# A new opening for an FFT-filter and feed-forward kernel: input by two queues, weight conversion in three steps, filter rows as 16 KB runs

One core of a Trainium2 chip. The metric is the device time of one execution in microseconds (us); lower is better. All runs quoted here are of the fast state (none had the lower clock or the longer time of the slow one), and every kernel's output was correct. Times of stages and of single waits come from one profiled execution of each kernel.

## The reference

```python
def _attn_ref(x, filt_r, filt_i):            # x (8, 3008, 256) f32; filters (1505, 256) f32
    X = np.fft.rfft(x, axis=1)
    Y = X * (filt_r + 1j * filt_i)[None, :, :]
    return np.fft.irfft(Y, n=x.shape[1], axis=1).astype(np.float32)

def _moe_ref(x, w_in, w_out):                # x (24064, 256); w_in (256, 2048), w_out (2048, 256): float64
    h = x @ w_in
    g = np.where(h > 0.0, h, np.exp(np.minimum(h, 0.0)) - 1.0)
    return (g @ w_out).astype(np.float32)

def reference(x, filt_r, filt_i, moe_w_in, moe_w_out):
    return _moe_ref(_attn_ref(x, filt_r, filt_i).reshape(8 * 3008, 256), moe_w_in, moe_w_out)
```

The weights arrive as float64. No engine multiplies them as such: the kernel takes the two 32-bit words of each number apart and builds a float32 ("conversion", sixteen pieces of 128x512 numbers).

## The kernel before

The length 3008 is 47 x 64, and the transform goes in two stages by matrix products. For each batch:

- x is read with its mirrored rows; VectorE makes sums and differences (`x_unit`), TensorE the first stage (`a_unit`), ScalarE evicts (copies the product from PSUM, where TensorE writes it, to SBUF), SyncE writes the result z to DRAM (`z_write`).
- z is read back, transposed on the way (`z_read`). In eight groups TensorE makes the second stage, VectorE multiplies by the filter (four products of 128x512), GpSimd adds the products in two sums, and TensorE goes back (`b_unit`, `bi_unit`).
- y goes through DRAM too, and after the "n-stage" (`n_unit`) the feed-forward loop runs over 192 "quads" of work, in which TensorE is full.

Batch 0 has nothing to hide behind: the *opening*. The same opening loads the whole filter into one tile `ff` and converts the weights. Its parts, with the lines "..." for what is cut:

```python
def x_load(b, c, queue=nc.sync, place=None):       # all on SyncE but the table
    ...
    queue.dma_start(w, ta_d[:, 2 * c:2 * c + 2, :])
    for h in range(2):
        ...
        nc.sync.dma_start(t[r]..., raw(x, b * N + i, [[N1 * D, 32], [32 * N1 * D, 2], [1, 2 * D]]))   # 2 KB runs
        for u in range(2):
            ...
            nc.sync.dma_start(t[r, :, u, :], raw(x, b * N + N1 - i - u, ...))                       # 1 KB runs, mirrored

def z_write(b, c):
    ...
    for r in range(2):
        nc.sync.dma_start(z[r], t[HALVES[r]])                                                       # 1 KB runs

def f_read_first(t, a):                            # the filter, by GpSimd's queue
    r = a * 64
    for c, src in enumerate((filt_r, filt_i)):
        nc.gpsimd.dma_start(t[r:r + 24, :, c, :, :]..., raw(src, 2 * a, [[64 * D, 24], [4 * D, NG], [1, 2 * D]]))  # 2 KB runs
        ...                                        # mirrored rows, 1 KB runs

def b_unit(b, g, f=None):
    ...
    nc.vector.tensor_tensor(out=sr, in0=re, in1=f[:, 0], op=ALU.mult)      # and si, p, q
    nc.gpsimd.tensor_tensor(out=sr, in0=sr, in1=p, op=ALU.subtract)
    nc.gpsimd.tensor_tensor(out=si, in0=si, in1=q, op=ALU.add)

def w_convert(k):                                  # one block
    nc.vector.tensor_scalar(out=m, in0=hi, scalar1=0x000FFFFF, ...)        # mantissa
    nc.scalar.activation(out=l, in_=lo, func=AXT.Identity, scale=2.0 ** -52)
    nc.scalar.activation(out=f, in_=m, func=AXT.Identity, scale=2.0 ** -20, bias=1.0)
    nc.vector.tensor_scalar(out=e, ...)            # three tensor_scalars: exponent
    ...
    nc.vector.scalar_tensor_tensor(out=e, ...)     # sign
    nc.vector.tensor_tensor(out=f, in0=f, in1=l, op=ALU.add)
    ...                                            # product, and four sums after every second piece

# the opening
for k in range(2):
    w_fetch(k)
for c in range(NXC):
    x_load(0, c, nc.scalar, ...)
nc.gpsimd.memset(ff, 0.0)
...
wait_x(3); w_fetch(2); w_fetch(3); wait_x(5)       # GpSimd held back until x is there
for a in range(2):
    f_read_first(ff, a)
for c in range(NXC):
    x_unit(0, c); a_unit(0, c); z_write(0, c)
    if c in (0, 2):
        w_convert(c // 2)
...                                                # z_read, then eight groups with w_convert(6..11) between
```

Of the kernel before, what the change touches and what calls it, by code (L numbers as in the profile page):

```python
# [22 lines left out]
N1 = 47  # L23
# [12 lines left out]
FBUFS = 3  # L36
LO, HI = slice(0, 48), slice(64, 112)
# [3 lines left out]
def _make_tables():  # L41










    n2, k2 = np.arange(N2), np.arange(K2)
    ta, tn = np.zeros((P, H, P)), np.zeros((P, H, P))
    for i in range(H):
        for h in range(2):
            if h and i == 0:
                continue
            n1 = N1 - i if h else i
            th = 2 * np.pi * (((N1 * n2[:, None] + n1) * k2[None]) % N) / N
            c, s = np.cos(th), -np.sin(th)  # L60
            c[:, 0], s[:, 0] = 1.0, 1.0 - 2.0 * (n2 % 2)
            sign = -1.0 if h else 1.0
            r = slice(h * 64, h * 64 + 64)
            for p, v in enumerate((c, sign * s, s, sign * c)):
                ta[r, i, p * 32:p * 32 + 32] = v
                tn[p * 32:p * 32 + 32, i, r] = v.T
    tb = ta.reshape(2, 2, 32, NXC, 2, 2, 4, 16, 2)[:, 0].transpose(3, 0, 1, 2, 4, 7, 5, 6)
    ta = np.ascontiguousarray(tb).reshape(P, H // 2, P)
    i = np.arange(H)[:, None]
    gb, gr, gi = (np.zeros((P, 2, 64)) for _ in range(3))  # L70
    q = np.arange(N1)[None]
    th = 2 * np.pi * ((i * np.where(q < 24, q, 70 - q)) % N1) / N1
    c, s = np.cos(th), np.sin(th)
    sign = np.where(q < 24, 1.0, -1.0)
    gb[0:24, 0, :N1], gb[24:48, 0, :N1] = c, s
    gb[64:88, 0, :N1], gb[88:112, 0, :N1] = c * sign, -s * sign
    for o in (0, 64):
        gr[o:o + N1, 0, 0:24], gr[o:o + N1, 0, 24:48] = 2 / N * c.T, 2 / N * s.T
        gi[o:o + N1, 0, 0:24], gi[o:o + N1, 0, 24:48] = 2 / N * (c * sign).T, -2 / N * (s * sign).T
    k1 = np.arange(24)[None]  # L80
    t0 = 2 * np.pi * ((i * k1) % N1) / N1
    t3 = 2 * np.pi * ((i * (32 + 64 * k1)) % N) / N
    c0, s0, c3, s3 = np.cos(t0), np.sin(t0), np.cos(t3), np.sin(t3)
    gb[0:24, 1, 0:24], gb[24:48, 1, 24:48] = c0, c3
    gb[64:88, 1, 24:48], gb[88:112, 1, 0:24] = -s3, -s0

    m0, m3 = np.full((24, 1), 2 / N), np.full((24, 1), 2 / N)
    m0[0] = m3[23] = 1 / N
    s0[:, 0] = s3[:, 23] = 0.0
    gr[0:24, 1, 0:24], gr[24:48, 1, 24:48] = m0 * c0.T, m3 * c3.T  # L90
    gi[0:24, 1, 24:48], gi[24:48, 1, 0:24] = -m0 * s0.T, -m3 * s3.T
    return [t.astype(np.float32) for t in (ta, tn, gb, gr, gi)]
# [8 lines left out]
def kernel(  # L101
# [41 lines left out]
    junk = glob.tile([P, 1], FP32, name="junk")  # L143
# [17 lines left out]
    def x_load(b, c, queue=nc.sync, place=None):  # L161

        t, w = place or (xp.tile([P, 2, 2, D], FP32, tag="xc", name="xc"), tap.tile([P, 2, P], FP32, tag="ta", name="ta"))
        xs[b, c], tas[b, c] = t, w
        queue.dma_start(w, ta_d[:, 2 * c:2 * c + 2, :])
        for h in range(2):
# [5 lines left out]
            for u in range(2):  # L172
                if i + u == 0:
                    nc.gpsimd.memset(t[r, :, 0, :], 0.0)
                else:
                    nc.sync.dma_start(t[r, :, u, :],  # L176
                                      raw(x, b * N + N1 - i - u, [[N1 * D, 32], [32 * N1 * D, 2], [1, D]]))
# [43 lines left out]
    def f_read_first(t, a):  # L221


        r = a * 64
        for c, src in enumerate((filt_r, filt_i)):
            nc.gpsimd.dma_start(t[r:r + 24, :, c, :, :].rearrange("q g u d -> q g (u d)"),
                                raw(src, 2 * a, [[64 * D, 24], [4 * D, NG], [1, 2 * D]]))
            for u in range(2):
                g0 = 1 if a == u == 0 else 0
                for r0, n in ((24, 16), (40, 7)):  # L230
                    nc.gpsimd.dma_start(t[r + r0:r + r0 + n, g0:NG, c, u, :],
                                        raw(src, 64 * (r0 - 23) - 4 * g0 - 2 * a - u,
                                            [[64 * D, n], [-4 * D, NG - g0], [1, D]]))
            if a == 0:
                nc.gpsimd.dma_start(t[24:48, 0, c, 0, :], raw(src, 32, [[64 * D, 24], [1, D]]))
# [244 lines left out]
    def w_fetch(k):  # L480
        q, j = divmod(k, 4)

        wd = wds[k] = wbufs[k % 5 if k < 12 else (2, 0, 1, 2)[k - 12]].bitcast(U32).rearrange("p c u d -> p (c u d)").rearrange("p (a w) -> p a w", w=2)
# [8 lines left out]
    def w_convert(k):  # L492
# [3 lines left out]
        q, j = divmod(k, 4)  # L496
        if j < 2:
            dst = w_in[q][:, 2 * j:2 * j + 2, :, :].rearrange("p j a c -> p a j c")
            shape = dict(a=2, j=2)
        else:  # L500
            dst = w_out[q][:, 0:4, j - 2, :]
            shape = None
        wd = wds.pop(k)
        lo, hi = wd[:, :, 0], wd[:, :, 1]
        m, e = (kp.tile([P, 512], U32, tag=t, name=n) for t, n in (("k0", "wm"), ("k1", "we")))
        fl = kp.tile([P, 2, 512], FP32, tag="c", name="wfl")
        f, l = fl[:, 0], fl[:, 1]

        nc.vector.tensor_scalar(out=m, in0=hi, scalar1=0x000FFFFF, scalar2=None, op0=ALU.bitwise_and)
        nc.scalar.activation(out=l, in_=lo, func=AXT.Identity, scale=2.0 ** -52)  # L510
        nc.scalar.activation(out=f, in_=m, func=AXT.Identity, scale=2.0 ** -20, bias=1.0)

        nc.vector.tensor_scalar(out=e, in0=hi, scalar1=20, scalar2=0x7FF,
                                op0=ALU.logical_shift_right, op1=ALU.bitwise_and)
        nc.vector.tensor_scalar(out=e, in0=e, scalar1=1151.0, scalar2=896.0, op0=ALU.min, op1=ALU.max)
        nc.vector.tensor_scalar(out=e, in0=e, scalar1=896.0, scalar2=8388608.0,
                                op0=ALU.subtract, op1=ALU.mult)
# [3 lines left out]
        if shape:  # L521
            f, e = (t.rearrange("p (a j c) -> p a j c", **shape) for t in (f, e.bitcast(FP32)))
        else:

            f, e = (t.rearrange("p (i a e s) -> p i e a s", i=2, a=4, e=2) for t in (f, e.bitcast(FP32)))
            dst = dst.rearrange("p (i e) (a s) -> p i e a s", i=2, a=4)
        if shape:
            nc.vector.tensor_tensor(out=dst, in0=f, in1=e, op=ALU.mult)
        else:
# [9 lines left out]

    def f_arrange():  # L540

        for c, src in enumerate((filt_r, filt_i)):
            for a in range(2):
                nc.gpsimd.dma_start(fd[:, a, 0:24, c, :, :].rearrange("g q u d -> q g (u d)"),
                                    raw(src, 2 * a, [[64 * D, 24], [4 * D, NG], [1, 2 * D]]))
                for u in range(2):
                    g0 = 1 if a == u == 0 else 0
                    nc.gpsimd.dma_start(fd[g0:NG, a, 24:47, c, u, :].rearrange("g q d -> q g d"),
                                        raw(src, 64 - 4 * g0 - 2 * a - u,
                                            [[64 * D, 23], [-4 * D, NG - g0], [1, D]]))  # L550
# [7 lines left out]
    with tc.manual_schedule():  # L558


        CONVERTS = {1: 6, 3: 7, 5: 8, 7: 9, 8: 10, 9: 11}
        with tc.tile_pool(name="boot", bufs=1) as bp:
            ff = bp.tile([P, NG, 2, 2, D], FP32, name="ff")
            wbufs += [bp.tile([P, 2, 2, D], FP32, name="wb%d" % i) for i in range(2)]
            more = [(bp.tile([P, 2, 2, D], FP32, name="xb%d" % i), bp.tile([P, 2, P], FP32, name="tb%d" % i))
                    for i in range(NXC - XBUFS)]

            def wait_x(c):

                nc.gpsimd.tensor_copy(out=junk[0:1], in_=xs[0, c][0:1, 0, 0, 0:1])  # L570

            for k in range(2):
                w_fetch(k)
            for c in range(NXC):
                x_load(0, c, nc.scalar, more[c - XBUFS] if c >= XBUFS else None)
            nc.gpsimd.memset(ff, 0.0)
            for t, d in ((gb, gb_d), (gr, gr_d), (gi, gi_d)):
                nc.gpsimd.dma_start(t, d)
            wait_x(3)
            w_fetch(2)  # L580
            w_fetch(3)
            wait_x(5)
            for a in range(2):
                f_read_first(ff, a)
            for c in range(NXC):
# [3 lines left out]
                if c in (0, 2):  # L589
                    w_convert(c // 2)  # L590
            for k in range(4, 7):
                w_fetch(k)
            for k in range(2, 6):
                w_convert(k)
                w_fetch(k + 5)
            z_read(0, 0)
            z_read(0, 1)
            for g in range(NG + 2):
                if g >= 2:
                    bi_unit(0, g - 2)  # L600
                if g < NG:
                    b_unit(0, g, ff[:, g])
                    if g + 2 < NG:
                        z_read(0, g + 2)
                if g >= 2:
                    y_write(0, g - 2)
                if g in CONVERTS:
                    w_convert(CONVERTS[g])
                if g == 1:
                    w_fetch(11)  # L610
                if g == 4:
                    w_fetch(12)
                if g in (5, 6):
                    x_load(1, g - 5)
# [5 lines left out]
        w_convert(12)  # L620
        nc.gpsimd.tensor_copy(out=junk[0:1], in_=t4s[0, 0][0:1, 0, 0:1])
        for k in (13, 14, 15):
            w_fetch(k)
        n_unit(0, 0)

# [8 lines left out]
        for c in range(2, XBUFS):  # L634
            at(c - 2, 0, x_load, 1, c)
        for k in (13, 14, 15):
            at(max(k - 14, 0), 1, w_convert, k)
# [3 lines left out]
        for b in range(B):  # L641
            t = (b - 1) * PER
            if b > 0:
                for c, s in enumerate((0, 2, 3, 4, 6, 7)):
# [78 lines left out]
```

## Time and profile before

| kernel before | value | how to read it |
|---|---|---|
| time | 2699.66 us (2699.26 to 2699.91, 4 runs) | median, in the rounds with the changed kernel |
| span of the profiled run | 2697.7 us, clock 0.977 | first to last instruction |
| TensorE busy | 96% | full from 185 us on |
| first product group | 72.4 us | when z (reread) and filter are both there |
| last of the first batch's products | 117.0 us | "stage" 44.6 |
| first n-stage matmul | 133.9 us | "tail" 16.9 |
| third n-stage matmul group | 223.0 us | "quads" 89.1 |
| from there to the end | 2474.7 us | "rest" |

The last five rows cut the span into pieces that can be compared between kernels: start of the first product group on VectorE (*first*), from there to the end of the last product (*stage*), to the first n-stage matmul (*tail*), to the third group of n-stage matmuls (*quads*), and the *rest*.

### The profile page before, as it was taken

What the parts mean: (1) busy time and instruction counts of PE and PEld (TensorE: products, weight loads), DVE (VectorE), ACT (ScalarE), POOL (GpSimd) and SP (SyncE); (2) the same over time, 40 slices, a digit from 0 to 9 for tenths busy, and PEclk for the clock granted to TensorE, in tenths of its full rate; (3) what the DMA queues carried; (4) which work ended last, traced back from release to release, by engine and by line L of the source; (5) the groups of instructions that cost most, each with busy time, mean ns of one, the idle gap of its engine ahead of it and who ended that gap; (6) DMA issues with size and microseconds to landing.
All of it is one profiled execution on the core that took longest, in us unless ns stands there. A gap on an engine that the chain in (4) does not pass through costs nothing.

```text
span 2697.7 us, 37154 instructions
## 1 busy us (share of the span) xinstructions
PE 2593.4 (96%) x13376; PEld 2196.4 (81%) x13376; DVE 1870.0 (69%) x3243; ACT 1474.7 (55%) x2561; POOL 279.9 (10%) x325
## 2 busy tenths in 40 slices
PE   1689999999999999999999999999999999999998
PEld 1278888987889878988889887898789888899887
DVE  4876776667667677767766677676767767666665
ACT  2255555555556555555555555565556555555554
POOL 4311210002100120001200021000210012000000
PEclk7589999999999999999999999999999999999999
DMA  9545331434213431153314332143421233110010
GB/s 232 156 121 132 79 78 40 101 77 104 62 38 89 103 96 38 45 124 79 85 37 91 90 90 70 38 101 83 114 58 38 60 87 92 38 40 19 21 27 16
DMA packets 234934, 208.23 MB, mean 77 GB/s; under 512 B 134052, under 2 KB 201142, under 8 KB 234752
## 3 DMA queue, kind: packets, MB, share of 16 engines
q1 hardware_dynamic: 216096, 168.15, 25.3%
q0 software_dynamic: 17792, 36.93, 5.6%
q8 instruction: 106, 1.74, 0.3%
q10 hardware_dynamic: 864, 0.79, 0.1%
q14 instruction: 76, 0.62, 0.1%
HBM read 130.68 MB, written 78.12 MB: 77 GB/s over the span
## 4 chain that ended last, share of the span: by engine, by line
PE 94%; DMA 2%; DVE 2%; issue 1%; SPq 0%; ACT 0%; POOL 0%; ACTq 0%; DVEq 0%; POOLq 0%
PE po L426 42%; PE phs L344 25%; PE phd L344 12%; PE pha L344 6%; PE psn L296 3%; PE pva L239 2%; PE psr L239 2%; PE psa L194 2%; DMA z<-t 0%; DMA ff<-in_filt_i_dram 0%; DMA ta<-ta_t 0%; PE pvb L239 0%; SPq L176 0%; DMA t<-z 0%; DMA xb<-in_x_dram 0%
## 5 line engine op out<-in xcount | busy, mean ns | idle before, releaser
L426 PE MATMUL po<-g,wo 128*128 128x256 f32 (+1 forms) x5376 | 1298.1, 376 | 0.0
L426 PEld LDWEIGHTS po<-g,wo 128*128 128x128 f32 x5376 | 1016.3, 190 | 129.4 <-issue 15.4
L355 ACT ACTIVATE g<-phs 128x512 f32<-128x512 f32 (+1 forms) x576 | 339.0, 589 | 845.3 <-PE phs L344 844.6
L352 DVE TENSOR_TENSOR g<-phd,g 128x512 f32<-128x512 f32 (+1 forms) x384 | 259.6, 676 | 462.8 <-ACT e L362 277.8
L362 ACT ACTIVATE e<-e 128x512 f32<-128x512 f32 (+1 forms) x768 | 477.3, 622 | 24.4
L344 PE MATMUL phs<-ys,wi 128*128 128x256 f32 (+1 forms) x1536 | 388.9, 376 | 11.2 <-ACT g L355 11.2
L344 PE MATMUL phs<-y,wi 128*128 128x256 f32 (+1 forms) x1536 | 395.5, 380 | 0.0
L366 DVE SCALAR_TENSOR_TENSOR g<-e,g 128x512 f32<-128x512 f32 (+1 forms) x576 | 387.2, 672 | 0.0
L361 ACT ACTIVATE e<-g 128x512 f32<-128x512 f32 (+1 forms) x576 | 352.8, 613 | 36.7 <-DVE g L352 30.6
L344 PEld LDWEIGHTS phs<-y,wi 128*128 128x128 f32 x1536 | 285.1, 190 | 82.9 <-ACT t L267 34.1
L344 PEld LDWEIGHTS phs<-ys,wi 128*128 128x128 f32 x1536 | 292.4, 191 | 45.4 <-ACT g L355 12.3
L366 DVE SCALAR_TENSOR_TENSOR g<-e,phs 128x512 f32<-128x512 f32 (+1 forms) x192 | 130.0, 677 | 139.6 <-ACT e L362 139.6
L256 POOL TENSOR_TENSOR sr<-sr,sp 128x512 f32<-128x512 f32 x64 | 81.2, 1269 | 1265.3 <-DVE sp L253 1265.3
L344 PE MATMUL phd<-ys,wi 128*128 128x256 f32 (+1 forms) x768 | 193.9, 375 | 1.8 <-DVE g L352 1.8
L344 PE MATMUL pha<-y,wi 128*128 128x256 f32 (+1 forms) x768 | 194.0, 375 | 0.0
L344 PE MATMUL phd<-y,wi 128*128 128x256 f32 (+1 forms) x768 | 193.9, 375 | 0.0
L361 ACT ACTIVATE e<-phs 128x512 f32<-128x512 f32 (+1 forms) x192 | 113.0, 588 | 140.5 <-PE phs L344 139.6
L344 PEld LDWEIGHTS phd<-ys,wi 128*128 128x128 f32 x768 | 145.7, 190 | 19.0 <-DVE g L352 2.6
L344 PEld LDWEIGHTS pha<-y,wi 128*128 128x128 f32 x768 | 146.3, 191 | 16.6
L344 PEld LDWEIGHTS phd<-y,wi 128*128 128x128 f32 x768 | 145.7, 190 | 17.2 <-issue 0.4
L406 DVE TENSOR_TENSOR g<-g,g 128x512 f32<-128x512 f32 (+1 forms) x192 | 130.7, 681 | 6.7
L403 DVE TENSOR_TENSOR g<-g,g 128x512 f32<-128x512 f32 (+1 forms) x192 | 130.7, 681 | 6.6
(111 smaller groups left out, 2377.6 us busy)
## 6 DMA issues: line engine op xcount, KB each, us to landing
z<-t SPq DMA_DIRECT2D x96, 256.0 KB
t<-z SPq DMA_DIRECT2D x256, 96.0 KB
yd<-t SPq DMA_DIRECT2D x128, 192.0 KB
t<-yd SPq DMA_DIRECT2D x192, 128.0 KB
f<-fd POOLq DMA_DIRECT2D x112, 192.0 KB, 3.7
out_dram<-o SPq DMA_DIRECT2D x640, 32.0 KB
tn<-tn_t SPq DMA_DIRECT2D x48, 256.0 KB
xc<-in_x_dram SPq DMA_DIRECT2D x92, 128.0 KB
```

What stands on the lines that cost most here:

```text
L239: nc.tensor.matmul(ps[:, u:u + w, :], table[k, v, :], rhs[k, u:u + w, :], start=True, stop=True)
L256: nc.gpsimd.tensor_tensor(out=sr, in0=sr, in1=p, op=ALU.subtract)
L296: nc.tensor.matmul(ps[:, ts(q, P)], t[:, i - 4 * m, ds(dh * P, P)], w[:, i - 4 * m, :], start=True, stop=True)
L344: nc.tensor.matmul(ps[:, a, 0:h], w_in[q][:, COMBO[n], a, :], y[n], start=start and a == 0, stop=True, skip_group_check=True)
L352: nc.vector.tensor_tensor(out=g[o], in0=i0, in1=i1, op=ALU.add)
L355: nc.scalar.activation(out=g[o], in_=i0, func=AXT.Copy)
L361: nc.scalar.activation(out=e, in_=src, func=AXT.Relu, scale=-1.0)
L362: nc.scalar.activation(out=e, in_=e, func=AXT.Exp, scale=-1.0)
L366: nc.vector.scalar_tensor_tensor(out=g[n], in0=es[n], scalar=1.0, in1=src, op0=ALU.subtract, op1=ALU.max)
L403: nc.vector.tensor_tensor(out=b12, in0=b22, in1=b12, op=ALU.subtract)
L406: nc.vector.tensor_tensor(out=g["t4"], in0=g["b21"], in1=g["t2"], op=ALU.subtract)
L426: nc.tensor.matmul(po[i][:, u, 0:h], w_out[q][:, COMBO[n], a, :], g[n][:, a, :], start=q == 0 and a == 0 and n in (1, 3, 6, 4), stop=True, ...
```

## The change

Its intent is to shorten the opening in three ways:

1. **Loading.** x's 1 KB rows go to GpSimd's queue, so that z's writes don't stand behind 35 x loads in SyncE's; the table comes in one DMA; ScalarE zeroes `ff`; GpSimd doesn't wait for x any more.
2. **Filter rows.** The order of k2 (the frequencies' second index) is permuted in the tables, so that neighbouring groups' frequencies lie side by side and a row of the filter is one run of 16 KB where it was eight of 2 KB.
3. **Conversion.** `w_convert` is cut in `w_split` (VectorE), `w_float` (ScalarE, now with the exponent: four activations for two) and `w_join` (VectorE), spread around the product groups and over the first quads.

```diff
+K2_ORDER = np.arange(K2).reshape(2, NG, 2).transpose(1, 0, 2).reshape(-1)
-    n2, k2 = np.arange(N2), np.arange(K2)
+    n2, k2 = np.arange(N2), K2_ORDER
 ...
-                    nc.sync.dma_start(t[r, :, u, :],
+                    queue.dma_start(t[r, :, u, :],
 ...
-            nc.gpsimd.dma_start(t[r:r + 24, :, c, :, :].rearrange("q g u d -> q g (u d)"),
-                                raw(src, 2 * a, [[64 * D, 24], [4 * D, NG], [1, 2 * D]]))
+            nc.gpsimd.dma_start(t[r:r + 24, c].rearrange("q k d -> q (k d)"), raw(src, 16 * a, [[64 * D, 24], [1, 16 * D]]))
 ...
+    def w_split(k):
+        nc.vector.tensor_scalar(out=m, in0=hi, scalar1=0x000FFFFF, scalar2=None, op0=ALU.bitwise_and)
+        nc.vector.tensor_scalar(out=e, in0=hi, scalar1=0x7FF00000, scalar2=None, op0=ALU.bitwise_and)
+    def w_float(k):
+        nc.scalar.activation(out=l, in_=wds[k][:, :, 0], func=AXT.Identity, scale=2.0 ** -52)
+        nc.scalar.activation(out=f, in_=m, func=AXT.Identity, scale=2.0 ** -20, bias=1.0)
+        nc.scalar.activation(out=ef, in_=e, func=AXT.Relu, scale=-8.0, bias=edges[:, 0:1])
+        nc.scalar.activation(out=e, in_=ef, func=AXT.Relu, scale=-1.0, bias=edges[:, 1:2])
 ...                                    # w_join: the rest of the old block
-            nc.gpsimd.memset(ff, 0.0)
+            nc.scalar.dma_start(tb, ta_d)
+            nc.scalar.memzero(ff)
-                x_load(0, c, nc.scalar, more[c - XBUFS] if c >= XBUFS else None)
+                x_load(0, c, (place, tb[:, 2 * c:2 * c + 2]), nc.gpsimd)
-            wait_x(3)
-            wait_x(5)
 ...
             for g in range(NG + 2):
+                k = {1: 4, 3: 5, 5: 6, 7: 7, 8: 8}.get(g)
+                if k:
+                    w_split(k)
 ...                                    # bi_unit, b_unit, z_read
+                if k:
+                    w_float(k)
 ...                                    # y_write
+                if k:
+                    w_join(k)
+        for j in range(7):
+            for k, fn in ((10 + j, w_float), (9 + j, w_join), (11 + j, w_split)):
+                if k < 16 and (k, fn) != (9, w_join):
+                    at(j // 2, j % 2, fn, k)        # over quads 0 to 3
```

## The prediction

> **What bounds the kernel now.** I read first the page's strip of 40 slices, then a table of stages made by asking busy times for stretches that I cut where the chain of waits changes hands, then the waits and the timeline of the opening.
>
> ```profile
> PE   1689999999999999999999999999999999999998
> PEclk7589999999999999999999999999999999999999
> DMA  9545331434213431153314332143421233110010
> ```
>
> One slice is 67 us. After slice 3 TensorE is full to the end, at full clock: nothing there can be won by this change, and the diff leaves that part as it is. The first 2.5 slices are the opening. The stages (columns: busy us and count of PE, PEld, DVE, ACT, POOL; then clock, DMA share, GB/s):
>
> ```profile
> 0.00:12.48 12.48, 0.00 (x0) 0.00 (x0) 0.00 (x1) 1.28 (x1) 10.46 (x11) 1.00 0.70 207
> 12.48:28.45 15.97, 6.81 (x48) 4.11 (x48) 11.76 (x22) 5.39 (x10) 2.39 (x5) 0.95 0.80 214
> 28.45:60.45 32.00, 5.79 (x48) 4.12 (x48) 13.87 (x29) 5.51 (x10) 16.80 (x30) 0.61 1.03 232
> 60.45:72.36 11.91, 4.00 (x14) 1.76 (x14) 8.73 (x18) 3.08 (x5) 1.80 (x4) 0.50 0.94 284
> 72.36:116.90 44.54, 34.84 (x116) 10.13 (x114) 37.40 (x60) 9.72 (x18) 20.67 (x19) 0.50 0.57 161
> 116.90:133.91 17.01, 3.38 (x9) 0.69 (x9) 16.39 (x34) 6.00 (x11) 3.60 (x5) 0.50 0.44 119
> 133.91:185.00 51.09, 39.83 (x207) 35.87 (x208) 39.60 (x80) 25.41 (x48) 1.75 (x4) 0.84 0.41 105
> 185.00:2697.00 2512.00, 2498.72 (x12939) 2139.72 (x12937) 1742.20 (x3005) 1418.28 (x2460) 222.39 (x250) 1.00 0.29 70
> ```
>
> Read by stage: to 72.36 the kernel loads x and the filter and writes and rereads z. The DMA engines bind; in the first 28 us they are 70 to 80% busy, from 28 to 60 full. From 72 to 134 is the filter stage of the first batch, with VectorE 37.4 of 44.5 and then 16.4 of 17.0 us busy: VectorE binds. From 134 to 185 are the first three steps of the feed-forward loop ("quads"), where TensorE loses 11.3 of 51.1 us. From 185 TensorE is 99.5% busy. Why z starts late is in SyncE's own queue:
>
> ```profile
> 9.89 0.31 SPq L169 DMA_DIRECT2D xc<-in_x_dram  x1
> 26.03 1.08 SPq L176 DMA_DIRECT2D xb<-in_x_dram  x2
> 28.45 19.53 SPq L208 DMA_DIRECT2D z<-t  x12
> ```
>
> All 35 x loads go through this queue, so the first z write, whose data was evicted at 17 us, is issued at 28.45. The queue stood until 9.89 for an earlier load; the compiled order of waits shows each hardware-queue DMA waiting for the completion of the one eight before it (SyncE and ScalarE together), and the software queue of GpSimd has eight places of its own. What VectorE does in the filter stage:
>
> ```profile
> 76.93 0.68 DVE L254 TENSOR_TENSOR sq<-psi,ff 128x512 f32<-128x512 f32 x1
> 77.53 1.12 DVE L509 TENSOR_SCALAR wm<-f 128x512 uint32<-128x512 uint32 x1
> 78.57 1.49 DVE L513 TENSOR_SCALAR we<-f 128x512 uint32<-128x512 uint32 x1
> 80.09 0.43 DVE L515 TENSOR_SCALAR we<-we 128x512 uint32<-128x512 uint32 x1
> 83.03 0.68 DVE L251 TENSOR_TENSOR sr<-psr,ff 128x512 f32<-128x512 f32 x1
> 87.61 0.69 DVE L251 TENSOR_TENSOR sr<-psr,ff 128x512 f32<-128x512 f32 x1 [2.11 <-PE psi L239]
> ```
>
> A weight conversion stands as one block of 5.5 us between two groups of four products; where none stands, the next group follows 4.58 us after the last (83.03 to 87.61), because the product frees a PSUM bank, TensorE refills it at half clock, and VectorE waits 2.11 us for it. Last, the waits: columns are total, times, longest.
>
> ```profile
> ACT wfl L511 <- DVE wm L509: 34.9, 6, 9.2
> ```
> ```profile
> PE phs L344 <- ACT g L355: 11.2, 3, 9.4
> ```
>
> ScalarE, in order, sits before a conversion's second activation until VectorE gets to it, and the evictions behind it wait too. The second is TensorE in the quads: one conversion block costs it 9.4 us.
>
> **What the Trainium skill says.** "DMA: Bandwidth & Descriptors", Issuing engines are not separate DMA queues: DMAs from all issuers share the same 16 engines, and several issuers save only issue time. The trace agrees where it is full (1.03 share, 232 GB/s), but before 28 us there is idle room to fill. Same page, Why small descriptors are slow: a fixed 3-cycle overhead per packet. From it I estimate 67 against 64 beats for a 2 KB run and 515 against 512 for 16 KB: some 4% of 1.57 MB, 0.3 us. No duration in this trace isolates it. "SBUF — State Buffer", Who interferes with whom: a tensor_scalar in a 2-port mode and a GpSimd instruction block each other entirely. The trace agrees: wm takes 0.42 us alone, 1.12 beside GpSimd's 128x512 product. "ScalarE: Activation LUTs", What ACT_TABLE_LOAD costs: 186 + 0.833 N ns, and 93 ns more for a bias from a tile. For N = 512 that is 612 ns; the trace has 628 to 666 for such activations.
>
> **The change part by part.**
>
> *Loading.* x's 1 KB rows (23 DMAs) go to GpSimd, the 2 KB rows (12) stay on SyncE, the table becomes one DMA. SyncE's twelve issues at 0.43 us are over by about 6 to 10 us, so z writes no longer stand behind x. GpSimd's 25 issues at 0.55 us take 14 us and end between 15 and 19, as its eight places allow. The memset of ff (6.9 us on GpSimd) becomes an activation of 8192 elements, an estimated 7.0 us by the formula above, from about 2.5 to 10 us, before ScalarE is needed. Bytes until the filter stage: x 3.1, z 3.1, filter 3.1, weights 2.1, tables 1.0 MB, together 12.4 MB. At 235 GB/s (stage three) from 2 us on this ends at 55 us; allowing for GpSimd's issue pace and z's first reread among it, the first product group starts at 56 where it was 72.36. By the other path: first eviction about 14 us, the last three each pending the z write three before (5.3 us apart in the old trace), so the last z write issued about 30 and landed about 41 (the old one took 13), reread 7 us, TensorE 4.6: 53. The later, 56, counts. **Gain 16.**
>
> *Filter rows.* 16 KB runs only shorten that list by 0.3 us; the mirrored rows stay at 1 KB. Later batches read through the rearranged copy, whose size does not change. Gain 0 by itself.
>
> *Conversion.* Two 0.46 us tensor_scalars leave VectorE; ScalarE has four activations, 2.4 us, for two. Six conversions instead of seven stand between the first products and the loop. Split (0.8, up to 2.5 beside GpSimd) now stands before a product group, where VectorE waits for a bank anyway; join (1.94) stands after, within the same 2.1 us; only the odd joins with their four sums (3.5 us) overrun. Starts of the groups: 2.4 + up to 1.6, 4.6, 4.9, 5.9, 4.9, 4.6, 4.9, and 2.4 for the last: 36.2 against 44.5. **Gain 8.** Between the last product and the first reading of yd, ScalarE's evictions now stand behind join 7 (3.6), split 8 and four activations: 7.4 us from product to evicted, where it was 9.2; with 7.8 to TensorE unchanged, 15.2 against 17.0. **Gain 2.**
>
> *Quads.* Three conversions in blocks become six in pieces, in quads 0 to 3. VectorE has some 6.3 us of own work in a quad of 10.5 (eleven operations of 0.57), the pieces add 3.7, 7.1, 6.4 and 3.6 us; ScalarE has 6.3 of its own and gets up to 4.8. Beside a single conversion nothing waits 9 us any more, but quads 1 and 2 are overfilled, and fetches 13 to 15 have half a quad to land in, where they took 6 to 8 us. I put the loss at 15 where it was some 18. **Gain 3.**
>
> Sum: 16 + 8 + 2 + 3 = 29, of 2699.9: 2671, said as 2670.
>
> **Rivals.** (1) *The loads are hidden no better*: the DMA engines are already full from 28 us, and the two queues only shift the queueing; weights 4 to 6 still push into z's reread. For: the share of 1.03 and the skill's sentence. Against: 7 us of idle DMA time before 28 (0.30 of 12.48 and 0.20 of 15.97). Then loading wins 5 to 8, the total 2680. (2) *ScalarE becomes the bound*: floats stand before evictions in its queue, and in the filter stage float 4 waits for a weight that is fetched behind the filter. For: old ScalarE waits in just this way. Against: 9.7 of 44.5 us busy. Then the filter stage wins nothing, quads lose 5 more: 2686. (3) *Everything unrolls*: z is done at 40, the filter at 48, quads run at TensorE's 40 us of 51: gains 22 + 10 + 4 + 9, total 2655.
>
> **Range and chances.** Rival 1 with half of 2 gives the upper end, 2687; rival 3 the lower, 2654. A gain of over 2% means below 2645.9, so 54 us, and even rival 3, with every stage at its best, sums to 45: 4%. Slower by 2% would need the loop itself to change: 1%.
>
> **What would show it.** Right: first z write issued at 13 to 16 us; first product near 56; last group done near 92; first n-stage matmul near 107; TensorE full from about 154 instead of 185, and the rest as long as before (2512 us). Wrong in loading: DMA share at 1.0 with the first product after 64. Wrong in conversion: VectorE idle before the joins for ScalarE, or products over 5.5 us apart on average. Wrong in the quads: TensorE idle over 15 us between the first n-stage matmul and full load. Wrong altogether: a difference after 200 us.

## The result

| | before | after |
|---|---|---|
| time, us | 2699.66 (2699.26 to 2699.91) | 2703.22 (2700.42 to 2704.09) |
| first | 72.4 | 78.2 |
| stage | 44.6 | 42.0 |
| tail | 16.9 | 16.4 |
| quads | 89.1 | 90.4 |
| rest | 2474.7 | 2475.4 |
| span | 2697.7 | 2702.3 |

The ratio is 1.0012, 95% interval 0.9994 to 1.0029: the same within 2%. (Ratios are the mean time of one kernel's fast runs over that of the other's of the same rounds, so not quite the ratio of the medians quoted.) That part of the forecast held, but the time lies 16 us above the range: the 29 us of gain are not there. All outputs are right.

The page's strip of 40 slices, kernel after:

```profile
PE   1589999999999999999999999999999999999998
PEclk7689999999999999999999999999999999999999
DMA  9555321424213431143313332143421233110010
```

From slice 3 on TensorE is full as before; whatever went wrong lies in the first three slices, 200 us. The stages of the kernel after (busy us and count of PE, PEld, DVE, ACT, POOL; then clock, DMA share, GB/s), cut where the same pieces of work begin:

```profile
0.00:15.91 15.91, 2.83 (x16) 1.46 (x16) 4.56 (x11) 11.95 (x9) 9.46 (x21) 1.00 0.89 245
15.91:32.60 16.69, 9.15 (x80) 6.11 (x80) 11.35 (x20) 8.45 (x16) 12.80 (x24) 0.87 0.96 257
32.60:71.94 39.34, 0.00 (x0) 0.00 (x0) 6.48 (x14) 4.82 (x8) 7.98 (x14) 0.50 0.94 174
71.94:78.16 6.22, 3.35 (x17) 2.11 (x20) 0.00 (x0) 0.00 (x0) 0.00 (x0) 0.50 0.41 126
78.16:120.16 42.00, 32.44 (x115) 8.91 (x108) 41.79 (x55) 17.29 (x30) 22.64 (x20) 0.74 0.52 151
120.16:136.55 16.39, 3.64 (x9) 0.68 (x9) 12.23 (x22) 6.04 (x11) 3.39 (x4) 0.50 0.56 152
136.55:185.00 48.45, 40.16 (x201) 35.36 (x202) 36.03 (x73) 31.34 (x58) 2.85 (x5) 0.85 0.50 132
185.00:2702.00 2517.00, 2500.34 (x12945) 2140.69 (x12943) 1749.54 (x3020) 1421.71 (x2468) 222.53 (x250) 1.00 0.29 70
```

The first two rows are what the change wanted: DMA shares of 0.89 and 0.96 where the first two stages of before had 0.70 and 0.80, all of x through the first stage by 32.6 us. The third row eats it: for 39 us TensorE does nothing, the DMA share is 0.94, and yet only 174 GB/s move, where stage three of before moved 232. SyncE's queue and the chain of waits say what it waits for (the queue: start, length, line, operation):

```profile
15.91 21.70 SPq L214 DMA_DIRECT2D z<-t  x12
71.94 17.26 SPq L220 DMA_DIRECT2D t<-z  x20
```
```profile
23.75 7.02 DMA z<-t
32.60 39.33 DMA z<-t
72.37 2.30 DMA t<-z
```

z's first write is issued at 15.91 instead of 28.45, and 22 us later all twelve are out. But the last, whose issue starts at 32.60, takes 39.33 us from there to land. In the kernel before the same link of the chain was

```profile
47.36 13.09 DMA z<-t
```

What shared the DMA engines with it is seen in the single DMA records of the trace (sorted here by size; not a view of the page): GpSimd's queue had moved the old runs of 1 and 2 KB joined to packets of mostly 4,096 bytes; now each forward row of the filter is one packet of 16,384, 96 in all.

```text
packets issued from GpSimd's queue, 24 to 66 us
kernel    bytes      n   mean ns
before     4096   1458       260
after      4096    994       324
after     16384     96      1679
```

z's packets have 1,024 bytes and took 65 ns on average before and 88 after (32 to 56 us), so little of the 39 us is their own.

### The profile page after: what moved, and what is told of

Same layout as the page of the kernel before. It is cut to its first block, busy times and chain, and to the rows that moved or that the text cites. A ratio compares the mean times of both kernels' runs of the same rounds, so it can differ in the third digit from the quotient of the medians.

```text
span 2702.3 us, 37137 instructions
## 1 busy us (share of the span) xinstructions
PE 2591.9 (96%) x13376; PEld 2195.3 (81%) x13376; DVE 1862.0 (69%) x3213; ACT 1501.6 (56%) x2594; POOL 281.6 (10%) x336
## 4 chain that ended last, share of the span: by engine, by line
PE 93%; DMA 3%; DVE 2%; ACT 1%; issue 0%; SPq 0%; DVEq 0%; ACTq 0%
PE po L430 42%; PE phs L348 24%; PE phd L348 12%; PE pha L348 6%; PE psn L300 3%; PE pva L243 2%; PE psr L243 2%; DMA z<-t 2%; PE psa L200 2%; DMA xc<-in_x_dram 0%; DVE wfl L534 0%; DMA xb<-in_x_dram 0%; ACT e L365 0%; DVE si L256 0%; DVE sq L258 0%
## 5 line engine op out<-in xcount | busy, mean ns | idle before, releaser
L260 POOL TENSOR_TENSOR sr<-sr,sp 128x512 f32<-128x512 f32 x64 | 81.3, 1270 | 1274.0 <-DVE sp L257 1274.0
```

## The experiments

Sixteen kernels were run. The expectations letter their theories, and say beside each letter what it holds; in short, A is the filter's 16 KB runs, C the sums on GpSimd that block VectorE, D the four activations in ScalarE's queue, E the weights in z's reread. Unless said otherwise each is compared with the kernel before in the same rounds on the same chip, whose median there was 2697.6 to 2698.2.

### Undoing the filter rows, and doing them alone

`e1`: the changed kernel with the old order and the old filter reads (with the order go the mirrored rows and the rearranged copy for later batches).

```diff
-K2_ORDER = np.arange(K2).reshape(2, NG, 2).transpose(1, 0, 2).reshape(-1)
+K2_ORDER = np.arange(K2)
-  nc.gpsimd.dma_start(t[r:r + 24, c]..., raw(src, 16 * a, [[64 * D, 24], [1, 16 * D]]))   # and the mirrored rows
+  nc.gpsimd.dma_start(t[r:r + 24, :, c, :, :]..., raw(src, 2 * a, [[64 * D, 24], [4 * D, NG], [1, 2 * D]]))
```

> The changed kernel with the old k2 order and the old filter reads (2 KB forward runs, 1 KB mirrored), all else as changed. Theory A (the 16 KB runs are what delays z: a 1 KB packet of the z write takes turns with packets of 16 KB that take 1.3 to 1.9 us each): the last z write, which took 39.3 us, lands in 10 to 15, the first product starts at 55 to 62 instead of 78.2, the time falls to about 2682 to 2688. Theory B (sharing the loads between two queues is what costs, the kind of filter row has no part): first product stays at 74 to 80, the time at 2700 to 2704.

`e2`: the kernel before with the new order and the 16 KB reads alone (the same edit the other way).

> The kernel before with only the new k2 order and the 16 KB filter runs. Theory A: z, written at the same time as the filter is read here too, lands later: first product at 82 to 92 instead of 72.4, time 2708 to 2720. Theory B: within 1 us of the kernel before, 2699 to 2701.

Measured: e1 2688.86 us (2688.7 to 2691.0), ratio 0.9966 [0.9952, 0.9981]; e2 2707.19 (2706.75 to 2707.28), ratio 1.0033 [1.0016, 1.0049]. The first product starts at 64.4 in e1 (78.2 in the changed kernel) and at 81.5 in e2 (72.4 before). So the filter rows put off the first product by 9 us in the old surroundings and by 14 in the new, and the rest of the change is worth some 9 us of the time. Both runs move the way of theory A, a little short of what it expected, and away from B. The chain of waits of e1:

```profile
32.76 18.63 DMA z<-t
52.58 9.68 DMA t<-z
```

z's last write, issued at nearly the same moment as in the changed kernel, lands after 18.63 us, not 39.33. In e2 the first product waits for z by a detour. z's reread is issued at 72.39, but before that ScalarE had waited 13.16 and 14.61 us for z writes to free its buffers, and the blocks of conversion behind those evictions keep VectorE busy until 81.4.

### What length of run

Four kernels keep the new order and change only how each 16 KB row is fetched. e3, e13 and e14 fetch it in two DMAs: interleaved pieces of 2 KB, of 4 KB, or two halves of 8 KB. e15 keeps 16 KB and cuts the DMA by rows, so that it has as many DMAs.

```diff
-  nc.gpsimd.dma_start(t[r:r + 24, c]..., raw(src, 16 * a, [[64 * D, 24], [1, 16 * D]]))
+  for o in range(2):                                                     # e3
+      nc.gpsimd.dma_start(..., raw(src, 16 * a + 2 * o, [[64 * D, 24], [4 * D, 4], [1, 2 * D]]))
+  for o in range(2):                                                     # e13
+      nc.gpsimd.dma_start(..., raw(src, 16 * a + 4 * o, [[64 * D, 24], [8 * D, 2], [1, 4 * D]]))
+  for o in range(2):                                                     # e14
+      nc.gpsimd.dma_start(..., raw(src, 16 * a + 8 * o, [[64 * D, 24], [1, 8 * D]]))
+  for q0, n in ((0, 16), (16, 8)):                                       # e15
+      nc.gpsimd.dma_start(..., raw(src, 16 * a + 64 * q0, [[64 * D, n], [1, 16 * D]]))
```

> The changed kernel, forward filter rows in the new order but each 16 KB run cut into 2 KB pieces by two interleaved DMAs; mirrored rows as changed. Theory A in its narrow form (the size of the packet): as e1, first product 55 to 62, time 2682 to 2688. Theory A in its wide form (the new order of the addresses, also in the mirrored rows, which is kept here, makes the reads slow): first product stays at 70 or later, time above 2694.

> The changed kernel, each 16 KB filter run cut into four 4 KB pieces in two interleaved DMAs (the run with 2 KB pieces had first product 68.2 us, 2693.9 us). If the length of the run does the damage (A2a): packets of 4 KB, first product at 66 to 70, 2690 to 2695, as with 2 KB. If the number of DMAs (A2b): the same, so this run alone tells nothing; it is the third point of the series of lengths.

> The changed kernel, each 16 KB filter run cut into two 8 KB runs in two DMAs. A2a, the length of the run: packets of 8 KB take over 0.6 us on average, first product between those of 4 KB and 16 KB, 70 to 75, 2695 to 2701. A2b, the number of DMAs: as with the 2 KB pieces, first product 66 to 70, 2691 to 2695.

> The changed kernel, 16 KB runs kept, each DMA cut by rows into 16 and 8. A2a, the length of the run: packets stay 16 KB and take 1.3 us or more, first product 75 to 80, 2699 to 2705, as the changed kernel (78.2, 2703.2). A2b, few packets in each DMA and few DMAs: more engines take part, first product 66 to 71, 2691 to 2696.

| | run | packet, bytes | last z write takes | lands at | first product | time, us | ratio, interval |
|---|---|---|---|---|---|---|---|
| e3 | 2 KB | 4,096 | 18.2 | 57.2 | 68.2 | 2693.89 | 0.9983 [0.9969, 0.9998] |
| e13 | 4 KB | 4,096 | 18.2 | 55.1 | 67.3 | 2691.81 | 0.9982 [0.9967, 0.9997] |
| e14 | 8 KB | 8,192 | 25.4 | 63.7 | 71.5 | 2696.14 | 0.9995 [0.998, 1.0009] |
| e15 | 16 KB, rows cut | 16,384 | 36.2 | 68.9 | 77.3 | 2702.68 | 1.0017 [1.0001, 1.0034] |
| after | 16 KB | 16,384 | 39.3 | 71.9 | 78.2 | 2703.22 | 1.0012 [0.9994, 1.0029] |

The landing of z, the first product and the time follow the length of the run, from 4 KB on, and not the number of DMAs (A2b falls: e15 is like the changed kernel). The intervals of neighbours overlap; those of e13 and e15 don't. Runs of 2 and 4 KB are alike, and the records show why that may be: both move in packets of 4,096 bytes. With them the new order is no better than the old one (e1: z lands at 51.4, first product 64.4, 2688.86). e3 met neither of its expectations: 68.2 and 2693.89 lie above the narrow form's 62 and 2688, and at the edge of the wide form's. So a small part of the loss, some 3 to 5 us, may belong to the new order itself or to its mirrored rows; no run separates this.

### Without z beside it

Does a long run harm z, or is it slow in itself? In e4 the filter goes through SyncE's queue, behind z's writes; in e10 it stays in GpSimd's, but a small read of z's last rows stands ahead of it, so that it starts when z has landed; e16 does the same with e13's 4 KB pieces.

```diff
 # e4                                          # in f_read_first, called behind z's writes
-            nc.gpsimd.dma_start(...)
+            nc.sync.dma_start(...)
 # e10, and e16 with 4 KB pieces                # behind the loop of z's writes
+            nc.gpsimd.dma_start(fbufs[0][0:4, 0], zs[0][20:24, 0:2, :])
+            for a in range(2):
+                f_read_first(ff, a)
```

> The changed kernel with the filter loads (16 KB runs kept) moved to SyncE's queue behind the z writes, so that both cannot take turns. Theory A: the last z write lands within 15 us; the filter follows in some 15 to 20 us; first product at 58 to 66, time 2684 to 2692. Theory B or reads that are slow in themselves at 9 GB/s an engine: z lands early but the filter only at 70 or later, first product 73 to 80, time 2698 to 2705.

> The changed kernel with its 16 KB filter runs kept on GpSimd's queue, but held back until z's last writes have landed (a small read of z's last rows stands before them in that queue). It tells two readings of the slow loading apart. Theory A1, only the taking of turns with z's small packets hurts: z lands near 43 us as in the run with the filter behind z (44.2), z's reread is issued near 44 and lands by 53 to 58 beside the filter, the 3.1 MB of the filter take 15 to 18 us from 43 and are there near 60, the first product group starts at 61 to 66 us (changed kernel 78.2), and the time is 2686 to 2692. Theory A2, reads in 16 KB runs are slow in themselves (about 120 GB/s as in the slices of the changed kernel): z lands at 43 too, but the filter takes 25 us or more from there, the first product starts at 70 us or later, and the time is 2695 or more.

> The run with the filter held back behind z, with each 16 KB run cut into 4 KB pieces in two interleaved DMAs. If reads in 16 KB runs are slow in themselves (A2), the filter lands by 60 to 68 us instead of 79.5 and the first product starts 6 to 12 us sooner than in the held run, at 61 to 67, with 2690 to 2697. If the late start is what cost the held run its gain, and the length only matters through the turns it takes from z, the first product stays at 71 to 74 and the time at 2702 to 2706.

e4: 2699.68 us, 1.0004 [0.9989, 1.0019]. z lands at 44.2, but SyncE, in order, must issue fourteen filter DMAs before z's reread, which it issues at 58.09. Its first product (74.1) and time lie in the range of "B or slow in themselves", but for this reason; it settles nothing about the length.

e10: 2705.84 us, 1.0027 [1.0012, 1.0042], first product 72.7; e16: 2704.67, 1.0019 [1.0002, 1.0035], first product 75.0. In both z has landed by 38 us. The end of the filter in the chain of waits, first of e10, then of e16:

```profile
41.65 17.71 DMA ff<-in_filt_i_dram
59.65 19.91 DMA ff<-in_filt_i_dram
```
```profile
46.18 18.56 DMA ff<-in_filt_i_dram
65.60 15.74 DMA ff<-in_filt_i_dram
```

The two end at 79.6 and 81.3; the first group of products waits for that with its second half, so the filter stage takes 48.5 and 47.9 us (42.0 in the changed kernel). After e10 I had read its slow filter as "16 KB reads are slow in themselves" (A2); e16, where nothing but the length differs (it ran on another chip, in other rounds), refutes that. Without z's writes beside it the filter is slow in either form, and e16's table of stages shows how:

```profile
40.00:44.00 4.00, 2.71 (x9) 1.16 (x11) 1.10 (x3) 0.00 (x0) 3.01 (x6) 0.50 1.04 143
44.00:48.00 4.00, 1.36 (x8) 0.51 (x3) 0.00 (x0) 0.00 (x0) 0.63 (x1) 0.50 1.06 97
48.00:52.00 4.00, 1.68 (x2) 0.00 (x1) 0.00 (x0) 0.00 (x0) 0.55 (x1) 0.50 1.05 119
```

A DMA share above 1.0 goes with 97 to 143 GB/s here; in the kernel before, from 60 to 64 us, a share of 1.02 went with 392. The share counts time in which a packet is under way, not bytes. Sorted by queue, the DMA records give the rates (GB/s, about 32 to 56 us):

```text
kernel                  GpSimd's queue   hardware queue   both
before                             123              108    232
e1, old rows                       124               70    194
e13, 4 KB                          121               66    188
e14, 8 KB                          125               65    190
e15, 16 KB, rows cut               108               61    169
after, 16 KB                       106               40    146
```

In this stretch GpSimd's queue moves 106 to 125 GB/s in all six kernels. What falls with 16 KB runs is the other queue, with z's writes (in e1 also the first rereads, from 52 us): 40 GB/s in the changed kernel, 65 to 70 in e1, e13 and e14. e15's 61 doesn't fit this average: there z falls behind only towards the end (2,500 of its 3,072 packets have started by 45.8 us, the last starts at 68.2).

That a long run harms z fits what the Trainium skill says in "DMA: Bandwidth & Descriptors", Queues, rings and completion order: each DMA engine goes round the queues that have work, and drains a whole packet of one before it turns to the next. A 16 KB packet of GpSimd's queue took 1679 ns (the 4,096-byte ones of before 260). From 32 to 56 us 2.1 z packets start to each data packet of GpSimd's queue in e1 and e13, and 2.2 in the changed kernel, where a packet may hold four times the bytes; but 2.6 in e14 and 3.4 in e15. The records don't name the engine, so they can't tell the turns. That the length does harm beside z's writes (e3 to e15) and none once they have landed (e10 against e16) is shown; that it is done by the turns is the page's mechanism, and not shown. Nor are 16 KB packets beside z all the time: the last starts at 57.4 us, and 519 of z's packets start after 60, beside the end of the filter and the weights, in packets of 4,096 bytes. The late z has run into the next load.

### The loading alone

`e9`: the kernel before with the new loading (x by two queues, table in one, `ff` zeroed by ScalarE, no waits for x), old rows, conversion in blocks.

```diff
-                x_load(0, c, nc.scalar, more[c - XBUFS] if c >= XBUFS else None)
-            nc.gpsimd.memset(ff, 0.0)
+            nc.scalar.dma_start(tb, ta_d)
+            nc.scalar.memzero(ff)
+                x_load(0, c, (place, tb[:, 2 * c:2 * c + 2]), nc.gpsimd)      # w_fetch(0), (1) among them
-            wait_x(3)                                                         # and wait_x(5)
```

> The kernel before with the new loading alone (x by two queues, the table as one DMA, ff cleared by ScalarE, no waits between x and the weights), its old rows and its old conversions in blocks. By the prediction, the conversion is worth 13 us of e1's gain, so this run at 2699 to 2702. By the traces (filter stage 2.2 us shorter, quads 2.1 us longer in e1) the conversion is worth nothing by itself: first product 63 to 66, time 2688 to 2692.

Measured: 2695.92 us (2694.84 to 2697.63), ratio 0.9994 [0.9977, 1.001]; first 67.3, stage 46.1, tail 17.0, quads 87.7. That lies between its two expectations and meets neither. The loading brings the first product 5 us forward. Set against e1, which adds the pieces of conversion: first 64.4, stage 42.3, quads 91.2. The pieces win some 3 us more in the loading and 4 in the filter stage, and lose some in the quads. How much is not sure: 87.7 to 89.1 in the three kernels with blocks, 88.3 to 91.2 in the eleven with pieces that leave the quads as they are in e1.

### The sums that block the joins

In the changed kernel VectorE's pieces stand where GpSimd adds the products of the group just done (VectorE, kernel after: the second half of one group and what follows):

```profile
84.87 0.68 DVE L258 TENSOR_TENSOR sq<-psi,ff 128x512 f32<-128x512 f32 x1
85.47 1.37 DVE L532 SCALAR_TENSOR_TENSOR we<-wb,we 128x512 uint32<-128x512 uint32 x1
86.76 1.75 DVE L534 TENSOR_TENSOR wfl<-wfl 128x512 f32<-128x512 f32 x1
88.55 0.69 DVE L539 TENSOR_TENSOR wi<-wfl,we 128x512 f32<-128x512 f32 x1
```

`e5` is e1 with the two sums of the first batch on VectorE (two more operations there, none on GpSimd).

```diff
-        nc.gpsimd.tensor_tensor(out=sr, in0=sr, in1=p, op=ALU.subtract)
-        nc.gpsimd.tensor_tensor(out=si, in0=si, in1=q, op=ALU.add)
+        eng = nc.vector if b == 0 else nc.gpsimd
+        eng.tensor_tensor(out=sr, in0=sr, in1=p, op=ALU.subtract)
+        eng.tensor_tensor(out=si, in0=si, in1=q, op=ALU.add)
```

> The kernel of the run e1 (old rows), with the two sums after each group of products in the first batch on VectorE in place of GpSimd. Theory C (the joins and splits, moved beside GpSimd's sums, are held up by them: 1.37 and 1.75 us in place of 0.69): joins go back to 0.69, splits to 0.42, VectorE has 1.2 us more per group; first to last product group 38.5 to 40 where e1 has 42.3; time 2684 to 2687. Rival (the joins are slow for another reason, such as their operands or ScalarE's writes): joins stay at 1.3 to 1.7 and the stage grows to 46 or more, time 2692 or more.

Measured: 2685.18 us (2683.48 to 2687.22), 0.9954 [0.9937, 0.997]. The same join in e5, with nothing on GpSimd beside it:

```profile
68.47 0.69 DVE L264 TENSOR_TENSOR si<-si,sq 128x512 f32<-128x512 f32 x1
69.07 0.69 DVE L535 SCALAR_TENSOR_TENSOR we<-wb,we 128x512 uint32<-128x512 uint32 x1
69.67 0.69 DVE L537 TENSOR_TENSOR wfl<-wfl 128x512 f32<-128x512 f32 x1
```

1.37 and 1.75 us become 0.69 each, and the splits 0.42 where they were 1.12 to 1.49. Although VectorE has sixteen operations more, the stage falls from 42.3 to 39.4. Theory C is shown.

### The activations in the quads

The chain of waits of the changed kernel shows one float's four activations (L521 to L526) ahead of an eviction, and TensorE behind it:

```profile
152.13 0.66 ACT wfl L521
152.79 0.52 ACT wfl L522
153.31 0.62 ACT we L525
153.93 0.02 issue
153.96 0.72 ACT we L526
154.68 0.44 ACT g L359
155.12 0.04 issue
155.16 1.86 PE phs L348 x4
```

`e6` is e1 with the exponent of conversions 10 to 15 on VectorE in the old form (two operations more there, two activations fewer).

```diff
+        if k >= 10:                                   # in w_split, in place of e's bitwise_and
+            nc.vector.tensor_scalar(out=e, in0=hi, scalar1=20, scalar2=0x7FF, ...)
+            nc.vector.tensor_scalar(out=e, in0=e, scalar1=1151.0, scalar2=896.0, ...)
+            nc.vector.tensor_scalar(out=e, in0=e, scalar1=896.0, scalar2=8388608.0, ...)
+        if k >= 10:                                   # in w_float, ahead of the last two activations
+            return
```

> The kernel of e1, with the exponents of conversions 10 to 15 (those in the quads) on VectorE as before the change, so that ScalarE has two activations for four there. Theory D (in the quads ScalarE is the bound, its four activations of 2.6 us stand ahead of the evictions): from the first to the third n-stage 85 to 88 us where e1 has 91.2; time 2683 to 2687. Rival (VectorE is the bound): 91 to 95, time 2689 or more.

Measured: 2687.34 us, 0.9959 [0.9944, 0.9973]; quads 91.2 to 88.9, less than expected. Even that may be scatter: e13 and e14, with all four activations, took 88.9 and 88.8. Another wait has come up in its chain: VectorE, which comes to batch 1's x sooner now, waits for its load.

```profile
141.15 4.10 DMA xc<-in_x_dram
```

`e12` tests that: `e11` (e5 and e6 together) with batch 1's x loads issued earlier.

```diff
+                if g in (5, 6):                       # among the groups of batch 0, as in the kernel before
+                    x_load(1, g - 5)
-        x_load(1, 0)
-        for c in range(1, XBUFS):
-            at(c - 2, 0, x_load, 1, c)
+        for c in range(2, XBUFS):
+            at(c - 3, 0, x_load, 1, c)
```

> Candidate for a version better than both: the changed kernel with the old k2 order and filter reads, the two sums of the first batch on VectorE, and the exponent of conversions 10 to 15 on VectorE (the run with all three remedies without the late weights, which had brought nothing). If the remedies don't add up because each uncovers the next wait (batch 1's x in the quads), the time is 2682 to 2686, as with the sums alone (2685) or all three (2684.5); if the late weights had cost the third run something, 2679 to 2682.

> The run before this one, with the first two x loads of batch 1 issued back in the filter stage (as in the kernel before the change) and the next two one quad earlier. If the wait for batch 1's x is what took the place of ScalarE's four activations in the quads, VectorE's wait on x near 140 us disappears, the stretch from the first to the third n-stage group falls from 88.9 us (exponent on VectorE) to 83 to 86, and the time is 3 to 6 us below the run before this one: 2677 to 2682. If the loads merely collide with y's writes and the weights, the stretch stays at 88 to 91 and the time the same within 2 us.

e11: 2684.73 us (2684.37 to 2686.47), 0.9951 [0.9936, 0.9966]; quads 91.4. e12: 2686.36 (2685.78 to 2690.4), 0.9961 [0.9944, 0.9978]; quads 89.2. The wait near 141 is gone, the time isn't. VectorE is by now nearly full (e12, the second and third 20 us of the quads; the third busy column is VectorE):

```profile
139.83:159.83 20.00, 15.40 (x89) 13.92 (x89) 18.56 (x39) 10.92 (x20) 2.32 (x4) 0.91 0.43 126
159.83:179.83 20.00, 15.29 (x88) 13.78 (x88) 19.39 (x40) 11.77 (x23) 4.41 (x4) 1.00 0.52 140
```

18.56 and 19.39 of 20 us busy. On ScalarE the exponent stands before evictions, on VectorE it fills VectorE; the stretch took 87.7 to 91.4 us in all the kernels. Theory D describes a wait that the chain shows; that taking it away gains anything is not shown. That VectorE binds in its place is read from its busy time; no run frees it.

### The weights in z's reread, and all together

`e7` is e1 with weights 5 and 6, and those behind them in the queue, fetched only after z's first rereads have landed; `e8` is e5, e6 and e7 in one.

```diff
-            for k in (4, 5, 6):
-                w_fetch(k)
-            for g in range(2):
-                z_read(0, g)
+            w_fetch(4)
+            for g in range(2):
+                z_read(0, g)
+            nc.gpsimd.tensor_copy(out=junk[64:65], in_=t2s[0, 1][64:65, 0, 0:1])
+            for k in (5, 6):
+                w_fetch(k)
```

> The kernel of e1, with the fetches of weights 5 to 8 held until z's first reread has landed. Theory E (the rest of the loading's miss, 64.4 where 56 was predicted, is the reread beside these fetches: 9.7 us for what 16 engines move in 4): reread 4 to 6 us, first product 59 to 62, time 2684 to 2687. Rival (the late weights hold up the conversions, or the reread is slow in itself): first product 63 to 66, or the filter stage longer by as much; time 2688 to 2692.

> e5, e6 and e7 together. If they add up: 2676 to 2681. If e7's late weights stall the conversions that e5 makes shorter: 2682 to 2686.

e7: 2688.46 us, 0.9961 [0.9945, 0.9978]; the reread takes 8.19 us for e1's 9.68, the first product starts at 62.2. Between the four kernels e1, e5, e6 and e7, whose loading is the same or nearly so, it starts at 61.2 to 64.4, so this is within the scatter, and e5 and e6, with the weights where they were, reread in 8.46 and 8.23: theory E falls. e8: 2684.49 us (2683.78 to 2685.89), 0.9949 [0.9934, 0.9964]. It, e5 and e11 can't be told apart; they are the fastest found, 13 us below the kernel before, and the gains of e5 and e6 don't add up.

## Why the prediction was wrong

| term | predicted | after | after with old rows (e1) |
|---|---|---|---|
| first (from 72.4) | 56 | 78.2 | 64.4 |
| stage (from 44.6) | 36.2 | 42.0 | 42.3 |
| tail (from 16.9) | 15.2 | 16.4 | 16.4 |
| quads, change | -3 | +1.3 | +2.1 |

**Filter rows: the step that failed.** The prediction has "16 KB runs only shorten that list by 0.3 us" and "Gain 0 by itself". The bytes were counted, and the queue beside them was not. The estimate took each 2 KB run for a packet, where the trace of before has packets of 4,096 bytes, and left z's writes out. The rows cost 9.2 us alone (2707.19 less 2698.02, e2) and some 12 in the changed kernel (its ratio less that of e1, 0.0046 of 2698). The page that I cited for the 3 cycles has the sentence on taking turns too, and the trace of before had the packets' durations (260 ns for 4,096 bytes): sixteen z packets' worth of bytes in one turn was there to be worked out. The prediction's test for a failure in loading, a DMA share at 1.0 with the first product after 64, is just what happened, but what it meant by it (rival 1, the engines full of bytes) did not: fewer bytes moved, 146 GB/s for 232 (32 to 56 us).

**Loading, gain 16.** z's first write at 13 to 16 us was right (15.91), and so was the pace of the evictions: the last z write is issued at 32.60 (said: 30). Without the long runs the gain is 8 in e1 and up to 11 in the kernels built on it. Two terms were mis-sized. The rate of 235 GB/s (its own line has 232) was taken from a stage in which z's packets and the filter's moved together; in e1 the two queues moved 194 from 32 to 56 us. And the last z write landed at 51.4, not 41; the reread behind it took 9.68, not 7. The later of the two paths was z's, and it ended at 64.4 where I had 53. Rival 1 had foreseen a gain of this size, 5 to 8.

**Conversion, gain 8: measured 2.6.** The join was put at 1.94 us "within the same 2.1 us". It takes 1.37 + 1.75 + 0.69 with overlaps, some 3.7, because of GpSimd's sums. For the splits the prediction had allowed for it ("up to 2.5 beside GpSimd"), for the joins it had not: the pages' rule that it cites covers one-input operations in fast modes, and another sentence of that section covers these (see below). (What ran beside them, GpSimd's "product" in the prediction, are the two sums.) The products came 5.64 us apart on average ((117.65 - 78.16) / 7; 6.02 before), over the 5.5 that it named as the sign of failure, for another reason than the wait on ScalarE that it gave.

**Tail, gain 2: 0.5. Quads, gain 3: none (1.3 longer, within the scatter told above).** Between the first and the third n-stage group TensorE stands idle 12.4 us (13.1 before), so the limit of 15 that I named was kept, and yet nothing was won. The block of 9.4 us is gone as said (the longest such wait is 5.7 now); six floats of 2.5 us in ScalarE's queue have taken its place, which is the wait of rival 2 in the quads: named, and given too little weight. How much of the missing 3 us it accounts for stays open (e6, e12).

**Right**: nothing changed after 200 us (rest 2475.4 for 2474.7), and zeroing `ff` on ScalarE took 7.03 us (estimated 7.0 by the skill's formula), the four activations of a float 0.52 to 0.73 each. Apart from the failed step, the gain would have been 9 (e1) of the 29 us: rivals 1 and 2 were both half true, and the estimate added up stages each at its best.

**Open**: how many turns z loses to one 16 KB packet; over how many of the 16 engines a DMA of 24, 16 or 7 rows is spread, which no record shows and e15 tests only in part; and why GpSimd's queue doesn't pass 125 GB/s in this stretch, and moves only some 82 in e16 (40 to 72 us), where only z's reread, with 37, goes beside it.

## What to carry to other kernels

A longer run isn't better when another queue is on the path: look at what packets stand beside it. Here a bulk load's runs of 4 KB did no more harm to small writes than runs of 2 KB, and runs of 8 KB did. A DMA share of 1.0 says that packets are under way, not that bytes move: read the GB/s beside it, by queue where you can. When work is cut into pieces and put into another engine's gaps, look up what runs on the neighbouring engine in just those gaps, and who stands behind the new pieces in the queue.

## What the Trainium skill lacked or had wrong

- "DMA: Bandwidth & Descriptors", Queues, rings and completion order, has the turns by whole packets, but neither it nor Rules for kernel authors (which asks for 1 MiB and more per DMA) warns that long runs hold up another queue's small packets: the last z write took 18.2 us beside runs of 2 and 4 KB, 25.4 beside 8 KB, 39.3 beside 16 KB.
- Same page, SWDGE vs HWDGE vs iDMA, gives a packet as preferably at most 4096 bytes. The trace has packets of 16,384 bytes from GpSimd's queue, at 1679 ns each beside z, one to each 16 KB run.
- "SBUF — State Buffer", Who interferes with whom, is right in saying that an operation of VectorE with two inputs in SBUF contends with GpSimd's reads; it gives no duration for such a pair. Here such an addition of 128x512 took 0.69 us alone and 1.75 beside GpSimd's sums.
